# Row halves that wait for TensorE's own semaphore, and the order inside an attention step

## The chip, the cores and the metric

The kernel runs on one core of a Trainium2 chip. TensorE multiplies matrices and writes to PSUM, ScalarE (ACT) and VectorE (DVE) read PSUM, GpSimd (POOL) works on SBUF alone, and SyncE (SP) issues most of the DMAs. Each engine works off its own queue in order and meets the others at semaphores. In the profile PE stands for matmuls and PEld for the weight loads in front of them. The metric is the device time of one execution in microseconds. Before the change it is 1590.65 us, the median of three runs (1590.64 to 1590.91).

## The reference, cut to what matters

```python
xn = layernorm(x)                                  # x: (1, 2048, 512)
qkv = xn @ A_wqkv                                  # 32 heads of 16
scores = einsum("bhqd,bhkd->bhqk", q, k) * 16 ** -0.5
p = softmax(scores)
s = (einsum("bhqk,bhkd->bhqd", p, v) -> (1, 2048, 512)) @ A_wo
g = silu(gelu(xn @ B_w1 + B_b1) @ B_w2 + B_b2)     # hidden width 1376
out = x + s * g
```

## The kernel before, in words

Operands of the dense products are split into a high and a low part, and each product is the sum of three (high by high, high by low, low by high), so that a contraction over 128 rows is many matmuls into one PSUM bank.

The work has two large parts. In the **dense part** (51 to 476 us) the products for q, k, v, the hidden layer and the gate are computed. Each contraction over 128 rows is cut into two of 64 rows. Row half 0 of TensorE's array takes the upper 64, row half 1 the lower 64, and matmuls of the two halves run side by side. A list named `plan` fixes the order: `quad` computes values, `half(j, 0)` and `half(j, 1)` compute a pair of hidden or query and key tiles (L590, weights w1), and `down` multiplies the hidden tiles by w2 (L590, weights w2). `run` takes one matmul for each half in turn. `fill` slips score matmuls (S, L183) among them, and VectorE takes the maxima of their rows (L189).

A bank is written by one half first and by the other afterwards, for instance `half(j, 0)` gives tile x to half 0 and `half(j, 1)` gives it to half 1. The second writer must wait until the first is done. `mm` keeps the last writer of each bank and a number `seen` up to which all matmuls are known to be done (a score matmul that waits for a free bank raises it too). Where that isn't enough, a **token** serves: `mark` puts a tiny ScalarE instruction on the queue (L604, tile junk, two of them on VectorE, L602) that waits for the latest matmul, and the matmul of the other half waits for the token. Tokens are put down ahead of need, in each `down` after its fourth pair of matmuls (`mark_early`) and at hooks in `quad`.

The **attention part** (476 to about 1550 us) has 512 steps, one for each 128 keys of a unit of four heads by 512 queries. A step has four T, one for each head: the scores, transposed (keys on partitions), by `t_one` at L739, each followed by an exp on ScalarE (L741). T take four banks in turn, three named pst and one named ps; the fourth T of a step takes ps. V at L804 multiplies the exps of the step before by the values, eight matmuls by column quarters. The row maxima for later units are computed beside this by S: one `S` writes a whole bank, `X` writes the left half of one and `Y` the right half; three banks are used in turn, and VectorE reduces each (L189). So a step in this mode has two `S`, one `X` and one `Y`. The string for it is `ORDER[3]`, used in all steps from the third to about the 490th:

```python
ORDER = {0: "TTTTV", 3: "STXTTSTYV"}
```

The first and second T of a step lie on row half 1, the third and fourth on row half 0 (L981); the first S and the X lie on half 0, the second S and the Y on half 1. So the first S and the first T share the array, and so do X and the second T, the third T and the second S, the fourth T and Y. Before Y stands a `nop` on TensorE that waits for X on TensorE's own semaphore, since both write the same bank from different halves.

Small jobs hang on the T of a step (`todo`, by step and position): what is put at position 0, after the first T, are `o_move` (five DMAs), `o_den` (a VectorE reciprocal L832 and two DMAs) and `o_div`; loads and the rest stand at position 3. When the maxima of a unit are complete, `s_end0` runs behind an S: a VectorE reduction (L247), two GpSimd instructions and the loads of a later unit's queries.

Of the kernel before, what the change touches and what calls it, by code (L numbers as in the profile page):

```python
# [8 lines left out]
F32 = mybir.dt.float32  # L9
F32R = mybir.dt.float32r  # L10
AF = mybir.ActivationFunctionType
# [25 lines left out]
FILL0 = 30  # L37
HB = 4
W2B = 2
ORDER = {0: "TTTTV", 3: "STXTTSTYV"}  # L40
HC = CH // 2
PAIRED = 28
KB = 3
# [5 lines left out]
def fused(ctx: ExitStack, tc: tile.TileContext, x, wqk, wv, wo, w1, b1, w2, b2, out):  # L49
    nc = tc.nc  # L50
# [17 lines left out]
    ident_r = keep.tile([P, P], F32R, name="ident_r")  # L68
# [17 lines left out]
    SYNC = mybir.DependencyInfo(mybir.DependencyClass.Sync, mybir.DependencyReason.DATA)  # L86
# [68 lines left out]
    done = {u: 0 for u in range(NU)}  # L155
# [106 lines left out]
    prog = {}  # L262
# [42 lines left out]
    for i in range(nu):  # L305
        pairs.append(ms[2 * i:2 * i + 2])
        if (i + 1) * len(qs) // nu > i * len(qs) // nu:
            g, c = qs[i * len(qs) // nu]
            pairs.append([("q", g, c), ("q", g, c + 1)])
    parts = [(c, f, h) for c in range(NCH) for f in range(FT) for h in range(2)]  # L310
    is_m = [pair[0][0] == "m" for pair in pairs]
    plan, nd = [("first", g, i) for g in range(VQ - 1) for i in (0, 2)], 0
    for j in range(len(pairs)):
        for h in range(2):
# [9 lines left out]
            n = 2 if nd < len(parts) and parts[nd][2] and ready - nd > room else 1  # L324
            n = max(n, need - 2 * (left - 1))
            while nd < ready and n > 0:
                c, f, k = parts[nd]
# [9 lines left out]
    def w1_load(j):  # L337
        if j < len(pairs):
            for u in pairs[j]:
                kind, n, f = u  # L340
                if kind == "m":
                    W1[u] = w_new(w1[f], 2, "raw1")
                elif f % 2 == 0:
                    W1[n] = w_new(wqk[:, n], 2, "raw1")

    def w1_split(j):
        if j < len(pairs):
            for u in pairs[j]:
                u = u if u[0] == "m" else u[1]
                if not isinstance(W1[u], tuple):  # L350
                    W1[u] = w_split(W1[u], "w1", 4)

    def w2_load(i):
        if i < len(ms):
            W2[ms[i][1:]] = w_new(w2[ms[i][2]], 2, "raw2")

    def w2_split(i):
        if i < len(ms):
            W2[ms[i][1:]] = w_split(W2[ms[i][1:]], "w2", W2B)
# [27 lines left out]
    def v_out(t, pv):  # L387
        dst = vsb[:, t, :H * VW].rearrange("p (h w) -> p h w", w=VW)[:, :, :DH]
        nc.scalar.activation(dst, pv.rearrange("p (h w) -> p h w", w=DH), AF.Copy)
# [148 lines left out]
    keep_r = ctx.enter_context(tc.tile_pool(name="keep_r", bufs=1, side="right"))  # L538
# [19 lines left out]
    writer = {}  # L558
    s_when, put, row = [], [0], [0, 0]
# [3 lines left out]
    def fill(a):  # L563
        due = FILL0 + put[0] + sum(made) * ROWS // (4 * LEAD)
        if sum(made) < 4 * LEAD and row[a] >= due and (made[0] <= made[1]) == (a == 0):
            taken()
            if later and later[0][0] <= 0:
                put[0] += 2
                u = later.pop(0)[1]
                s_end1(u)  # L570
                s_end2(u)
                return
            s_one(a)
            row[a] += 1
            tick()
# [6 lines left out]

    def mm(a, key, ps, lhs, rhs, first, last):
        r = slice(64 * a, 64 * a + 64)
        token = None
        if not first and writer[key][0] != a and writer[key][1] > prog["seen"]:
            if not tokens or tokens[-1][0] < writer[key][1]:
                mark()
            prog["seen"], token = next(x for x in tokens if x[0] >= writer[key][1])
        i = nc.tensor.matmul(ps, lhs[r], rhs[r], start=first, stop=last).ins  # L590
        if token is not None:
            tc.add_manual_dep(i, token, SYNC, reason="other row tile")
        prog["pe"] += 1
        row[a] += 1
        latest[0] = (prog["pe"], i.name)
        writer[key] = (a, prog["pe"])

    tokens, latest = [], [None]

    def mark(dve=False):  # L600
        if dve:
            i = nc.vector.tensor_copy(junk[:, 1:], ident_r[:1, :1].bitcast(F32)).ins  # L602
        else:
            i = nc.scalar.activation(junk[:, :1], ident_r[:1, :1].bitcast(F32), AF.Copy).ins  # L604
        tc.add_manual_dep(i, latest[0][1], SYNC, reason="row tile done")
        tokens.append((latest[0][0], i.name))

    def mark_early(n):
        if prog["seen"] < n:
            mark()  # L610

    junk = keep_r.tile([1, 2], F32, name="junk")

    def run(ops, hooks={}):
        for n, two in enumerate(zip(*ops)):
            prog["n"] += 1
            for a in range(2):
                fill(a)
                mm(a, *two[a])
            for h in hooks.get(n, []):  # L620
                h()
# [3 lines left out]
    def terms(u, a, begin):  # L625
        kind, n, f = u
        c = f if kind == "q" else n
        out = []
        for k in range(KT):
            for i, j in ((0, 0), (0, 1), (1, 0)):  # L630
                if kind == "v":
                    lhs, rhs = (xh, xl)[i][c][:, k, f * P:(f + 1) * P], (wv_h, wv_l)[j][:, k]
                else:
                    w = W1[u if kind == "m" else n]
                    lhs, rhs = w[i][:, k * P:(k + 1) * P], (xh, xl)[j][c][:, k]
                out.append([u, PH[u], lhs, rhs, False, False])
        if begin:
            out[0][4] = True
        else:
            out[-1][5] = True  # L640
        return out
# [3 lines left out]
    def down(c, f, part):  # L645
        i = c * FT + f
        if f == 0 and part == 0:
            PA[c] = [ps_v.tile([P, D], F32, name="pv")] + [ps_t.tile([P, D], F32, name="pst") for t in range(3)]
        h, w = HS[c, f], W2[c, f]
        side = (part + i) % 2  # L650
        ops = [[], []]
        for a in range(2):
            for t in ((0, 1), (2, 3))[(a + side) % 2]:
                ts = slice(t * P, (t + 1) * P)
                for n, (x, y) in enumerate(((0, 0), (0, 1), (1, 0))):
                    ops[a].append(((c, t), PA[c][t], h[x][:, ts], w[y],
                                   f == 0 and part == 0 and n == 0, f == FT - 1 and part == 1 and n == 2))
        n = prog["pe"]
        if (c, f, part) == parts[-2]:
            run(ops, {2: [lambda: mark(True)], 5: [lambda: mark(True)]})  # L660
        else:
            run(ops, {3: [lambda: mark_early(n)]})
        if part == 0:
            w2_split(i + 1)
            w2_load(i + 3)
            return
        del HS[c, f], W2[c, f]
        if f == FT - 1:
            for t in (0, 2, 1, 3):
                gt = wk.tile([P, D], F32, name="gt", bufs=4)  # L670
                if c == NCH - 1:
                    nc.vector.tensor_add(gt, PA[c][t], b2_sb)  # L672
                else:
                    nc.scalar.activation(gt, PA[c][t], AF.Copy)
                rs = slice(c * CH + t * P, c * CH + (t + 1) * P)
                if c < NCH - 1:
                    chores.append((gt, rs))
                else:
                    nc.gpsimd.dma_start(g_d[rs, :], gt)
# [22 lines left out]
    def quad(n, at):  # L702
        us = first[n]
        for u, b in zip(us, BANKS[n]) if at == 0 else ():
            pool, name = {"x": (ps_x, "ps"), "m": (ps_m, "ps"), "v": (ps_v, "pv"), "t": (ps_t, "pst")}[b]
            PH[u] = pool.tile([P, CH], F32, name=name)
        for i in range(at, at + 2):
            hooks = {6: [mark]} if i in (1, 2) else {}
            if n == VQ - 2 and i in (0, 2):
                hooks[3] = [lambda: w1_split(0) if i == 0 else w1_load(1)]  # L710
            run((terms(us[i], 0, i < 2), terms(us[(i + 2) % 4], 1, i < 2)), hooks)
            if i >= 2:
                for u in (us[i - 2], us[i]):
                    v_out(u[1] * NCH + u[2], PH.pop(u))
# [213 lines left out]
    for u in range(NU):  # L928
        g, c = divmod(u, NCH)
# [17 lines left out]
    for t in range(NW):  # L947
        n = DONE + 2 * t
# [6 lines left out]
    for i, t in enumerate(late):  # L955
        n = L - 2 * len(late) - 1 + 2 * i
# [9 lines left out]
    for n in range(L + 1):  # L966
        ua, ka = divmod(n, 16)
        want = due(n) - due(n - 1)
        i = 0
        for op in ORDER[want] if n > 1 else ("TTTTV", "TTSTSVT")[n]:  # L970
            if op in "SXY":
# [67 lines left out]
```

## Time and profile before

| | |
|---|---|
| median of the runs | 1590.65 us |
| the profiled execution | 1590.04 us |
| its span, first to last instruction | 1588.3 us |
| granted TensorE clock | 1.00 throughout |
| dense part | about 51 to 476 us |
| attention steps with S | about 478 to 1500 us |
| ScalarE busy in 900 to 1100 us | 198.17 us of 200 |
| VectorE busy in 900 to 1100 us | 183.02 us of 200 |

A row of the timeline gives start, length, engine, line, operation, output<-inputs, and, in brackets, how long the engine was idle ahead of it and what ended that. Neighbouring rows of one kind are merged (x2, x3). A wait row gives the total, the number and the longest. PE's busy time counts a matmul from its start to a modelled end, with the filling and emptying of the array, and these overlap from one matmul to the next.

### The profile page before, as it was taken

How to read it: one execution, taken by the hardware profiler on the slowest of the kernel's cores; microseconds unless marked ns; L12 is line 12 of the kernel's file. 1: busy time of each engine (PE TensorE's matmuls, PEld its weight loads, DVE VectorE, ACT ScalarE, POOL GpSimd, SP SyncE). 2: the span in 40 equal slices, each digit the busy share in tenths (PEclk: the TensorE clock that was granted, in tenths of full speed). 3: DMA queues.
4: the chain of work that ended last, by engine and by line, in shares of the span. 5: the costliest groups of instructions: out<-in, count | busy, mean ns of one | idle time of the engine just before them, and what ended most of it. 6: DMA issues, size and time to landing. Idle time of an engine off the chain costs nothing.

```text
span 1588.3 us, 31761 instructions
## 1 busy us (share of the span) xinstructions
PE 1581.8 (100%) x12144; PEld 934.7 (59%) x12144; DVE 1379.1 (87%) x2261; ACT 1259.1 (79%) x2520; POOL 373.7 (24%) x394
## 2 busy tenths in 40 slices
PE   9999999999999999999999999999999999999998
PEld 8899999999894444444444444444444444444445
DVE  7599898989889999999999999999999999999734
ACT  4334343434349999999999999999999999999984
POOL 4145575756640011001000100100100000000143
PEclk9999999999999999999999999999999999999999
DMA  6626343454332123112410511411150111110252
GB/s 206 150 59 161 109 137 99 157 139 134 114 96 59 37 42 59 28 38 47 76 31 25 70 41 30 62 39 29 33 76 21 32 29 36 36 29 22 59 192 101
DMA packets 74648, 116.87 MB, mean 74 GB/s; under 512 B 23012, under 2 KB 24292, under 8 KB 73320
## 3 DMA queue, kind: packets, MB, share of 16 engines
q1 hardware_dynamic: 70748, 101.89, 23.7%
q0 software_dynamic: 3264, 12.35, 4.5%
q8 instruction: 96, 1.57, 0.4%
q10 hardware_dynamic: 484, 0.60, 0.1%
q14 instruction: 56, 0.46, 0.1%
HBM read 84.35 MB, written 25.97 MB: 69 GB/s over the span
## 4 chain that ended last, share of the span: by engine, by line
PE 97%; ACT 1%; DVE 1%; issue 0%; DMA 0%; ACTq 0%; DVEq 0%
PE pv L804 33%; PE ps L183 24%; PE ps L590 12%; PE pst L739 10%; PE pst L590 7%; PE ps L739 3%; PE ps L80 3%; PE pv L590 2%; PE ps L458 1%; ACT slot L741 1%; PE pst L80 1%; DVE st L417 0%; PE pst L440 0%; DMA xt<-in_x 0%; PE pst L458 0%
## 5 line engine op out<-in xcount | busy, mean ns | idle before, releaser
L189 DVE TENSOR_REDUCE mx<-ps 128x2 f32<-128x512 f32 x2048 | 1299.5, 684 | 144.6 <-PE pst L739 35.2
L741 ACT ACTIVATE slot<-pst 128x512 f32<-128x512 f32 x1533 | 831.7, 614 | 17.8 <-PE pst L739 9.6
L804 PE MATMUL pv<-slot,vsb 128*32 128x512 f32 x4096 | 545.4, 605 | 0.0
L183 PEld LDWEIGHTS ps<-kt,slot 48*128 48x128 f32 x1364 | 223.8, 184 | 280.2 <-DVE mx L189 278.3
L183 PE MATMUL ps<-kt,slot 48*128 48x512 f32 x1364 | 379.4, 365 | 0.0
L739 PE MATMUL pst<-qt,kt 50*128 50x512 f32 x1149 | 376.0, 436 | 0.5 <-DVE gt L672 0.3
L741 ACT ACTIVATE slot<-ps 128x512 f32<-128x512 f32 x515 | 316.5, 615 | 2.5 <-PE ps L183 0.2
L590 PE MATMUL ps<-slot,w1h 64*128 64x512 f32 x1088 | 218.1, 393 | 0.0
L739 PEld LDWEIGHTS pst<-qt,kt 50*128 50x128 f32 x1149 | 188.6, 184 | 41.8 <-ACT slot L865 12.6
L183 PE MATMUL ps<-kt,qz 48*128 48x512 f32 x512 | 212.7, 415 | 0.0
L183 PEld LDWEIGHTS ps<-slot,slot 48*128 48x128 f32 x598 | 98.3, 184 | 121.5 <-DVE mx L189 120.7
L183 PE MATMUL ps<-slot,slot 48*128 48x512 f32 x598 | 166.0, 364 | 0.0
L739 PE MATMUL ps<-qt,kt 50*128 50x512 f32 x387 | 162.7, 422 | 0.0
L590 PEld LDWEIGHTS ps<-slot,w1h 64*128 64x128 f32 x1088 | 151.5, 185 | 8.4 <-ACT junk L604 2.6
L804 PEld LDWEIGHTS pv<-slot,vsb 128*32 128x32 f32 x4096 | 80.8, 108 | 109.2 <-issue 100.2
L590 PE MATMUL ps<-slot,w1l 64*128 64x512 f32 x544 | 141.9, 393 | 0.0
L377 POOL TENSOR_TENSOR hl<-hg,hh 128x512 fp32r<-128x512 f32 x76 | 96.8, 1295 | 129.7 <-ACT hh L376 85.9
L250 POOL CAST nmh<-nm 128x16 fp32r<-128x16 f32 x32 | 6.3, 196 | 477.4 <-DVE nm L247 409.3
L739 PE MATMUL pst<-qt,slot 50*128 50x512 f32 x384 | 113.4, 421 | 0.0
L604 ACT ACTIVATE junk<-ident_r 1x1 f32<-1x1 f32 x92 | 18.0, 196 | 116.5 <-PE pst L590 113.3
L183 PEld LDWEIGHTS ps<-kt,qz 48*128 48x128 f32 x512 | 93.8, 183 | 16.3
L842 POOL TENSOR_TENSOR ot<-ot,dn 64x512 f32<-64x512 f32 x15 | 19.6, 1304 | 299.7 <-DMA dn<-den_d 256.9
(159 smaller groups left out, 1757.7 us busy)
## 6 DMA issues: line engine op xcount, KB each, us to landing
raw<-in_w SPq DMA_DIRECT2D x88, 256.0 KB
qk_h<-hh SPq DMA_DIRECT2D x32, 256.0 KB
qk_l<-hl SPq DMA_DIRECT2D x32, 256.0 KB
qt<-qk_h SPq DMA_DIRECT2D x128, 64.0 KB
slot<-qk_h SPq DMA_DIRECT2D x92, 64.0 KB
g_d<-gt POOLq DMA_DIRECT2D x16, 256.0 KB, 3.5
qt<-qk_l SPq DMA_DIRECT2D x64, 64.0 KB
dn<-den_d SPq DMA_DIRECT2D x32, 128.0 KB
```

What stands on the lines that cost most here:

```text
L80: nc.tensor.matmul(ps, lhs[a], rhs[b], start=first and n == 0, stop=last and n == 2)
L183: return nc.tensor.matmul(ps[:, c0:c0 + w], QS[u][r, p, qi * P:(qi + 1) * P], kts[u // NCH % KB][p][r, k0:k0 + w], start=True, stop=True).ins
L189: nc.vector.tensor_reduce(MX[u][:, 2 * p:2 * p + 2, qi, ki][:, heads, parts], ps.rearrange("p (n c) -> p n c", c=HC), axis=AX.X, op=OP.max)
L250: nc.gpsimd.tensor_copy(hl[:, 0], nm)
L377: nc.gpsimd.tensor_sub(hl, raw, hh.bitcast(F32))
L458: nc.tensor.matmul(pq["q", g, c], W1[g][i][:, k * P:(k + 1) * P], (xh, xl)[j][c][:, k], start=n == 0 and k == 0, stop=n == 2 and k == KT - 1)
L590: i = nc.tensor.matmul(ps, lhs[r], rhs[r], start=first, stop=last).ins
L604: i = nc.scalar.activation(junk[:, :1], ident_r[:1, :1].bitcast(F32), AF.Copy).ins
L739: nc.tensor.matmul(ps, kts[g % KB][p][r, k * P:(k + 1) * P], QT[u][r, p, :], start=True, stop=True)
L741: nc.scalar.activation(PT[u, k][:, 2 * p + a, :], ps, AF.Exp, scale=SCALE)
L804: nc.tensor.matmul(PV[u][32 * j:32 * j + 32, :], vsb[:, k, h:h + 32], PT[u, k][:, j, :], start=(k == 0), stop=(k == NT - 1))
L842: eng.tensor_mul(ot[c][rs, g // 2], ot[c][rs, g // 2], DN.pop(u)[rs])
```

## The change

Tokens disappear. Where a matmul must wait for the other half, a `nop` on TensorE waits for the bank's last writer on TensorE's own semaphore; `seen` then rises to that writer and not to a later matmul. `mark`, `mark_early`, the tile junk and all hooks that put tokens down go. Apart from that, the first T and the first S of a step change places in `ORDER[3]`.

```diff
-ORDER = {0: "TTTTV", 3: "STXTTSTYV"}
+ORDER = {0: "TTTTV", 3: "TSXTTSTYV"}
...
-        token = None
         if not first and writer[key][0] != a and writer[key][1] > prog["seen"]:
-            if not tokens or tokens[-1][0] < writer[key][1]:
-                mark()
-            prog["seen"], token = next(x for x in tokens if x[0] >= writer[key][1])
+            hold = nc.tensor.nop().ins
+            tc.add_manual_dep(hold, writer[key][2], SYNC, reason="other row tile")
+            prog["seen"] = writer[key][1]
         i = nc.tensor.matmul(ps, lhs[r], rhs[r], start=first, stop=last).ins
-        if token is not None:
-            tc.add_manual_dep(i, token, SYNC, reason="other row tile")
         prog["pe"] += 1
         row[a] += 1
-        latest[0] = (prog["pe"], i.name)
-        writer[key] = (a, prog["pe"])
+        writer[key] = (a, prog["pe"], i.name)
...
-        n = prog["pe"]
-        if (c, f, part) == parts[-2]:
-            run(ops, {2: [lambda: mark(True)], 5: [lambda: mark(True)]})
-        else:
-            run(ops, {3: [lambda: mark_early(n)]})
+        run(ops)
...
-            hooks = {6: [mark]} if i in (1, 2) else {}
+            hooks = {}
```

More of the change, by code (lines that the diff above doesn't have):

```diff
@@ L584, in mm @@
         r = slice(64 * a, 64 * a + 64)
-        token = None
         if not first and writer[key][0] != a and writer[key][1] > prog["seen"]:
-            if not tokens or tokens[-1][0] < writer[key][1]:
-                mark()
-            prog["seen"], token = next(x for x in tokens if x[0] >= writer[key][1])
+            hold = nc.tensor.nop().ins
+            tc.add_manual_dep(hold, writer[key][2], SYNC, reason="other row tile")
+            prog["seen"] = writer[key][1]
         i = nc.tensor.matmul(ps, lhs[r], rhs[r], start=first, stop=last).ins
-        if token is not None:
-            tc.add_manual_dep(i, token, SYNC, reason="other row tile")
         prog["pe"] += 1
         row[a] += 1
-        latest[0] = (prog["pe"], i.name)
-        writer[key] = (a, prog["pe"])
[L598 to L602, printed above, removed]
-        else:
[L604 to L612, printed above, removed]
+        writer[key] = (a, prog["pe"], i.name)
     def run(ops, hooks={}):
@@ L657, in down @@
                                    f == 0 and part == 0 and n == 0, f == FT - 1 and part == 1 and n == 2))
-        n = prog["pe"]
-        if (c, f, part) == parts[-2]:
-            run(ops, {2: [lambda: mark(True)], 5: [lambda: mark(True)]})
-        else:
-            run(ops, {3: [lambda: mark_early(n)]})
+        run(ops)
         if part == 0:
```

## The prediction

> **What bounds the kernel now.** I read the page first, then the waits, then one stretch of the timeline in each of the two parts that the change touches.
>
> ```profile
> PE 1581.8 (100%) x12144; PEld 934.7 (59%) x12144; DVE 1379.1 (87%) x2261; ACT 1259.1 (79%) x2520; POOL 373.7 (24%) x394
> ...
> PE pv L804 33%; PE ps L183 24%; PE ps L590 12%; PE pst L739 10%; PE pst L590 7%; PE ps L739 3%; PE ps L80 3%; PE pv L590 2%; PE ps L458 1%; ACT slot L741 1%; PE pst L80 1%; DVE st L417 0%; PE pst L440 0%; DMA xt<-in_x 0%; PE pst L458 0%
> ...
> L604 ACT ACTIVATE junk<-ident_r 1x1 f32<-1x1 f32 x92 | 18.0, 196 | 116.5 <-PE pst L590 113.3
> ```
>
> The page says that TensorE is the bound everywhere, but a matmul's end in it is modelled, so it cannot tell a packed step from one that is held up. The last row is the token: 92 tiny ScalarE instructions, 18.0 us busy, with ScalarE idle 116.5 us ahead of them. ScalarE is not on the chain in that part, so neither figure is a saving. What the tokens cost TensorE stands in the waits (total us, times, longest):
>
> ```profile
> PEld ps L183 <- DVE mx L189: 399.0, 476, 0.8
> ...
> PEld ps L590 <- ACT junk L604: 2.6, 9, 0.4
> ```
>
> Nine waits, 2.6 us. The 399 us above them look like the thing to attack, and are not: 476 times 0.84 us, in which the weight-load path has nothing to load while the eight value matmuls (L804) run. The attention steps show it. Here are two and a half of them, by timeline (start, length, engine); the windows row ahead counts 490 such steps in 1021.92 us, 2.086 us each.
>
> ```profile
> 478.50:1500.42 1021.92, 1021.81 (x7858) 460.96 (x7854) 934.84 (x1536) 1011.37 (x1991) 75.87 (x126) 1.00 0.20 41
> ```
>
> ```profile
> 899.90 0.50 PE L183 MATMUL ps<-kt,slot 48*128 48x512 f32 x1
> ...
> 899.91 0.62 ACT L741 ACTIVATE slot<-ps 128x512 f32<-128x512 f32 x1
> ...
> 900.58 0.18 PEld L739 LDWEIGHTS ps<-qt,kt 50*128 50x128 f32 x1
> ...
> 900.71 0.28 PE L183 MATMUL ps<-kt,slot 48*128 48x256 f32 x1
> ...
> 901.01 1.06 PE L804 MATMUL pv<-slot,vsb 128*32 128x512 f32 x8
> 901.92 0.62 ACT L741 ACTIVATE slot<-ps 128x512 f32<-128x512 f32 x1
> ...
> 902.01 0.50 PE L183 MATMUL ps<-kt,slot 48*128 48x512 f32 x1
> ...
> 902.01 0.73 PE L739 MATMUL pst<-qt,kt 50*128 50x512 f32 x2
> ...
> 902.35 0.27 PE L183 MATMUL ps<-kt,slot 48*128 48x256 f32 x1
> ...
> 902.55 1.89 DVE L189 TENSOR_REDUCE mx<-ps 128x2 f32<-128x512 f32 x3 [0.22 <-PE ps L183]
> 902.58 0.40 PE L183 MATMUL ps<-kt,slot 48*128 48x512 f32 x1
> 902.58 1.57 ACT L741 ACTIVATE slot<-pst 128x512 f32<-128x512 f32 x3
> 902.59 0.18 PEld L739 LDWEIGHTS ps<-qt,kt 50*128 50x128 f32 x1
> 902.68 0.18 PEld L183 LDWEIGHTS ps<-kt,slot 48*128 48x128 f32 x1
> 902.71 0.38 PE L739 MATMUL ps<-qt,kt 50*128 50x512 f32 x1
> 902.82 0.28 PE L183 MATMUL ps<-kt,slot 48*128 48x256 f32 x1
> ...
> 903.03 1.06 PE L804 MATMUL pv<-slot,vsb 128*32 128x512 f32 x8
> ...
> 904.02 0.50 PE L183 MATMUL ps<-kt,slot 48*128 48x512 f32 x1
> ...
> 904.49 0.18 PEld L183 LDWEIGHTS ps<-kt,slot 48*128 48x128 f32 x1
> ...
> 904.60 0.41 PE L183 MATMUL ps<-kt,slot 48*128 48x512 f32 x1
> ```
>
> Steps begin at 899.90, 902.01 and 904.02: 2.11 us, then 2.01 us. From the value matmuls to the next step it is 1.00 us (901.01 to 902.01) and 0.99 us (903.03 to 904.02), so the start of a step waits for nobody. The difference sits in front of the value matmuls: 1.11 us in the long step, 1.02 us in the short one. What is late there is the fourth T, which writes the bank ps. In the long step its weights load at 900.58. The exp that empties this bank ran from 899.91 for 0.62 us, to 900.53, and 0.05 us later the load starts. In the short step the exp ended at 902.54 and the load came at 902.59, which is 0.58 us into the step and just in time. So every second step is held by a loop through ScalarE: first T, its exp, three more exps behind it, then the fourth T of the next step. VectorE is close behind, but has 0.22 us of idle time per step at 902.55.
>
> **The change, part by part: the order in a step.** S and T of a step's first pair lie on different row halves and start together at 902.01, S first in the queue. They don't hand over together. VectorE, idle before, takes S at 902.55, 0.54 us after the start; ScalarE takes T at 902.58, after 0.57 us. This is not a property of ScalarE, as a step without S shows, where a T comes first and ScalarE was idle:
>
> ```profile
> 1530.65 0.73 PE L739 MATMUL pst<-qt,kt 50*128 50x512 f32 x3
> ...
> 1531.19 1.58 ACT L741 ACTIVATE slot<-pst 128x512 f32<-128x512 f32 x3 [0.16 <-PE pst L739]
> ```
>
> 0.54 us again. So the second of two that end together reports 0.03 us later, and the swap turns this round: T's exp comes 0.03 us earlier, S's reduction 0.03 us later. The Trainium skill, page "TensorE: Matmul & The Clock Gate", section "The cost: per-tile semaphore tail", says that completions which each raise a semaphore are written one after another, 26.3 ns each beside 4.7 ns for a further tile; by it the second would be 31 ns late, an estimate from the page, and 245 such gains would make 7.6 us. The trace agrees, at 0.03 us.
>
> What 0.03 us is worth follows from the loop. It closes once in two steps, from a first T to the fourth T of the step after, so a pair of steps (4.12 us now, against 2 x 2.01 = 4.02 us if nothing held it) gets shorter by 0.03 us, as 0.10 us is more than 0.03. 490 steps are 245 pairs: 245 x 0.03 = 7.4 us.
>
> Against it stands VectorE. Its three reductions run from 902.55 for 1.89 us, to 904.44; the second S of the next step, whose bank they free, loads weights at 904.49 and starts at 904.60, 0.58 us into the step, the same place as 902.58 in the short step. It comes just in time, and with reductions 0.03 us later it starts at 0.61. The half-width S behind it stands at 0.81 us (900.71; 902.82) and would stand at 0.84. In the short step 0.21 us lie between it and the value matmuls (902.82, 903.03), so these could start at 0.84 + 0.21 = 1.05 us. The fourth T lets them start at 1.11 - 0.03 = 1.08 us. So the ScalarE loop still ends last, by 0.03 us. That fails where VectorE has one more thing to do:
>
> ```profile
> L247 DVE TENSOR_REDUCE nm<-mx 128x16 f32<-128x128 f32 x32 | 8.8, 276 | 0.1
> ```
>
> Some 30 pairs hold such a reduction of 0.276 us, and there I count no gain: 30 x 0.03 = 0.9 us given back. Bounds for the order: VectorE takes all of it (0) to all 245 pairs gaining (7.4). I take 7.4 - 0.9 = 6.5 us.
>
> The moved T brings its queue work with it: the exp, and in some steps what hangs on the first T, which are o_move's five DMAs and o_den's reciprocal and two DMAs. On SP they now stand ahead of the query loads that a first S may ask for; on VectorE the reciprocal stands ahead of the first reduction, in the 0.22 us of idle time. Nothing on PE waits for these within the step, so I cost them at nothing; without that cover each would delay one reduction by its own length. The half-width X now stands right behind the S of its own half; it starts 0.34 us after it in any case (902.01, 902.35), a few ns either way.
>
> **The dense part.** The trace has nine token waits. The order of the changed program has twelve holds (a TensorE no-op that waits for TensorE's own semaphore) in place of twelve tokens that a matmul waited for; the other 80 tokens were never waited for. One wait, and beside it an undisturbed stretch:
>
> ```profile
> 160.85 0.39 PE L590 MATMUL pst<-w2h,hl 64*128 64x512 f32 x1
> ...
> 161.09 0.39 PE L590 MATMUL pst<-w2h,hl 64*128 64x512 f32 x1
> 161.12 0.20 ACT L604 ACTIVATE junk<-ident_r 1x1 f32<-1x1 f32 x1 [2.12 <-PE pst L590]
> ...
> 161.38 0.18 PEld L590 LDWEIGHTS ps<-slot,w1h 64*128 64x128 f32 x1 [0.33 <-ACT junk L604]
> ...
> 161.72 0.39 PE L590 MATMUL ps<-slot,w1h 64*128 64x512 f32 x2
> ...
> 185.03 0.53 PE L590 MATMUL pst<-w2h,hl 64*128 64x512 f32 x2
> 185.26 0.53 PE L590 MATMUL ps<-slot,w1h 64*128 64x512 f32 x2
> ```
>
> Undisturbed, a half starts a matmul every 0.23 us (185.03, 185.26). Here the half that was behind goes from 161.09 over 161.38 to 161.72, 0.63 us for two such slots of 0.46: 0.17 us lost. The half that was ahead, from 160.85, loses 0.41 us. Nine waits cost 1.5 to 3.7 us; I take 1.5, since the half that is behind ends last.
>
> A hold waits for the last matmul of the other half on that bank itself, not for a token put behind later work: seven pairs back in nine of the twelve, 7 x 0.23 = 1.6 us, against a matmul of 0.39 us. So it finds its semaphore raised. The same construct stands before the second half-width S already: the first starts at 902.35, ends after 0.27 us, and the weights behind the no-op load at 902.68, 0.06 us later, while the matmul begun at 902.58 is still going on. It doesn't empty the array. If a hold cost what a token did, this gain would be 0. Behind a hold stands all of TensorE's queue, but it has the other fourteen matmuls still to issue from. ScalarE's 18.0 us and the two VectorE tokens are off the chain: nothing.
>
> Sum, against this execution's 1590.04 us (span 1588.3): -6.5 - 1.5 = -8.0, so 1582.0. The median of the runs is 0.6 higher, 1590.65: 1582.6 us.
>
> **The rivals.** (1) The 0.03 us belongs to the row half, not to the place. S is always on the first half there, and 1530.65 has no S beside it, so no row excludes it. Then T gains nothing: -1.5, 1589.2 us. The same page of the Trainium skill, section "What overlaps and what doesn't", has matmuls start and end strictly in program order, which speaks for the place; no run here shows a pair the other way round. (2) VectorE takes half of the gain: its slack of 0.03 us is no more than the step, so where steps scatter, it ends last. -3.3 - 1.5: 1585.9 us. (3) The slower one: the later reductions push the second S in each long step, and the value matmuls follow the half-width S there and not the fourth T. It decides once the half-width S stands within 0.21 us of the value matmuls; then each pair loses 0.03 us, +7.4 - 1.5 = +5.9: 1596.5 us. Against it: in the long step they are 0.30 us apart (900.71, 901.01), 0.09 us of room for 0.03. (4) The holds do not do what they say and stall as the tokens did: -6.5, 1584.1 us, inside the range.
>
> **How the numbers follow.** Forecast, with (4): 0.60. (2): 0.18. (1): 0.14. (3): 0.08. The likeliest is 1582.6 us, by itself 1579.5 (all pairs, and 3.7 in the dense part, are -11.1) to 1584.5. For 8 in 10 I go to 1588.0, past (2) and short of (1). A change under 0.2%, 3.2 us, cannot be told from none: faster 0.78, same 0.14, slower 0.08.
>
> **What would show it.** First exp of a step 0.54 us after its T where ScalarE was idle, first reduction 0.57 us after its S; long steps of 2.08 us and short ones still 2.01; the stretch of 490 steps near 1015.4 us; no wait of weight loads on ScalarE in the dense part. Wrong, if long steps stay at 2.11 (1), or if the second S starts 0.61 us or later into most steps and the value matmuls move with it (2, 3).

## The result, and the profile after

The changed kernel takes 1582.61 us, median of six runs (1582.34 to 1583.08), against 1590.64 us (1590.40 to 1590.91) for the kernel before on the same chip: a ratio of 0.9950, 95% interval 0.9937 to 0.9963, or 8.0 us less. The profiled execution took 1582.56 us, its span is 1580.8 us (1588.3 before).

The waits of the whole execution (total us, times, longest), as far as weight loads wait for ScalarE's exps:

```profile
PEld pst L715 <- ACT slot L717: 310.0, 404, 0.8
...
PEld ps L715 <- ACT slot L717: 107.2, 139, 0.8
```

The wait for a ScalarE token is gone from the list, and so is the 399 us wait of S for VectorE. The latter has for the most part only changed its name: the weight loads ahead of the first matmul of a step have nothing to do while the value matmuls run, 0.84 us in most steps (479 of the 543 waits in the two rows are 0.8 us or longer), and the first matmul is a T now. Since it moved to another name with the order of two instructions, this was no wait for the engine named.

The two parts by windows (stretch, its length, then busy us of PE, PEld, DVE, ACT, POOL with their instructions), the 490 attention steps and the dense part from its first to its last row-half matmul; below them the dense part of the kernel before:

```profile
478.00:1492.98 1014.98, 1014.87 (x7858) 472.03 (x7855) 936.98 (x1536) 1009.52 (x1991) 75.85 (x126) 1.00 0.21 41
51.82:474.94 423.12, 423.12 (x3560) 387.36 (x3560) 373.02 (x585) 147.12 (x270) 238.10 (x209) 1.00 0.42 121
```

```profile
51.56:475.53 423.97, 423.97 (x3561) 386.23 (x3560) 373.12 (x587) 160.69 (x361) 239.03 (x209) 1.00 0.42 120
```

The steps lost 1021.92 - 1014.98 = 6.94 us, the dense part 0.85 us. The dense part began 0.26 us later in this execution (51.82 against 51.56), before anything that the change touches, and the three add up to the 7.5 us of the spans within 0.1 us (6.94 + 0.85 - 0.26 = 7.53).

A long and a short step after the change, by timeline:

```profile
884.38 0.62 ACT L717 ACTIVATE slot<-ps 128x512 f32<-128x512 f32 x1
...
884.42 0.49 PE L715 MATMUL pst<-qt,kt 50*128 50x512 f32 x1
...
884.42 0.50 PE L183 MATMUL ps<-kt,slot 48*128 48x512 f32 x1
...
884.91 0.18 PEld L183 LDWEIGHTS ps<-kt,slot 48*128 48x128 f32 x1
884.95 1.57 ACT L717 ACTIVATE slot<-pst 128x512 f32<-128x512 f32 x3
884.99 0.42 PE L183 MATMUL ps<-kt,slot 48*128 48x512 f32 x1
885.05 0.18 PEld L715 LDWEIGHTS ps<-qt,kt 50*128 50x128 f32 x1
...
885.25 0.27 PE L183 MATMUL ps<-kt,slot 48*128 48x256 f32 x1
...
885.48 1.06 PE L780 MATMUL pv<-slot,vsb 128*32 128x512 f32 x8
...
886.47 0.50 PE L715 MATMUL pst<-qt,kt 50*128 50x512 f32 x1
...
886.47 0.50 PE L183 MATMUL ps<-kt,slot 48*128 48x512 f32 x1
...
887.00 1.57 ACT L717 ACTIVATE slot<-pst 128x512 f32<-128x512 f32 x3
887.04 1.89 DVE L189 TENSOR_REDUCE mx<-ps 128x2 f32<-128x512 f32 x3 [0.17 <-PE ps L183]
...
888.49 0.50 PE L715 MATMUL pst<-qt,kt 50*128 50x512 f32 x1
```

T starts at 886.47 and its exp at 887.00, after 0.53 us; S starts at the same time and its reduction follows after 0.57 us (887.04). The two have exchanged their delays. The steps last 2.05 us (884.42 to 886.47) and 2.02 us. In the long one the load of the fourth T still waits for the exp on its bank (884.38 + 0.62 = 885.00, load at 885.05), but 0.63 us into the step, not 0.68. The second S loads at 0.49 us, as soon as VectorE has freed its bank.

The two steps are typical. Each score matmul (T, S, X or Y) adds one to a semaphore of TensorE when it is done, and the trace has the times of these updates: the two of a first pair come 0.034 us apart in the median of 488 steps, before and after the change, and 0.034 to 0.035 us in nine steps of ten. In the median of the steps the first exp started 0.566 us after its T before, and 0.533 us after the change.

### The profile page after: what moved, and what is told of

It is laid out like the page before. It is cut to its first block, busy times and chain, and to the rows that moved or that the text cites. A ratio compares the mean times of both kernels' runs of the same rounds, so it can differ in the third digit from the quotient of the medians.

```text
span 1580.8 us, 31627 instructions
## 1 busy us (share of the span) xinstructions
PE 1573.9 (100%) x12144; PEld 946.8 (60%) x12144; DVE 1381.3 (87%) x2259; ACT 1243.7 (79%) x2428; POOL 372.7 (24%) x394
## 4 chain that ended last, share of the span: by engine, by line
PE 98%; DVE 1%; DMA 0%; issue 0%; ACT 0%; DVEq 0%
PE pv L780 33%; PE pst L715 22%; PE ps L589 12%; PE ps L183 9%; PE pst L589 7%; PE ps L715 7%; PE ps L80 3%; PE pv L589 2%; PE ps L458 1%; PE pst L80 1%; DVE st L417 0%; PE pst L440 0%; DMA xt<-in_x 0%; PE pst L458 0%; DVE slot L75 0%
## 5 line engine op out<-in xcount | busy, mean ns | idle before, releaser
L370 ACT ACTIVATE hg<-ps,b_sb 128x512 f32<-128x512 f32 x44 | 27.8, 684 | 133.6 <-PE ps L589 122.1
L715 PEld LDWEIGHTS ps<-qt,kt 50*128 50x128 f32 x387 | 71.1, 184 | 45.6 <-ACT slot L717 39.9
```

The lines of the kernel that those rows point to most:

```text
L370: nc.scalar.activation(raw, ph.pop(u), AF.Gelu_apprx_tanh, bias=b1_sb[:, u[2]:u[2] + 1])
L715: nc.tensor.matmul(ps, kts[g % KB][p][r, k * P:(k + 1) * P], QT[u][r, p, :], start=True, stop=True)
```

## The experiments

Each was compared with the kernel before on the same chip; the ratio has its 95% interval.

**The order alone.**

```diff
-ORDER = {0: "TTTTV", 3: "STXTTSTYV"}
+ORDER = {0: "TTTTV", 3: "TSXTTSTYV"}
```

> The order of the step alone, tokens as before. If the order carries its share of the forecast, this is 6.5 to 7.5 us under before (490 steps near 1014.4 us instead of 1021.9), and the first exp of a step starts 0.53 to 0.54 us after its T. Rival: the order is worth 0.8 us or less and the two changes only work together; then it is within 1 us of before.

Measured: 1583.02 us, ratio 0.9955 (0.9942 to 0.9967), 7.3 us under before (1590.31). The steps by windows:

```profile
478.46:1493.34 1014.88, 1014.78 (x7859) 472.13 (x7855) 936.92 (x1536) 1009.34 (x1991) 75.90 (x126) 1.00 0.21 41
```

The order alone carries the 7 us, with tokens as before. The rival, that the two changes only work together, falls.

**The holds alone.** The changed kernel with `3: "STXTTSTYV"`.

> The holds alone, order of the step as before. By the forecast 1.5 us under before; by the trace of the changed kernel, in which the dense part from its own start is 0.84 us shorter, 0.8 us. The 490 steps stay at 1021.9 us. Rival: a token wait costs 0.3 to 0.4 us each, and something gives a part back: then 2.6 to 3.7 us, or a stretch of the dense part that is longer than before.

Measured: 1589.55 us, ratio 0.9995 (0.9986 to 1.0004), 0.8 us under before. The interval holds 1, so the time alone shows nothing; the dense part in the trace does, 423.07 us against 423.97:

```profile
51.48:474.55 423.07, 423.07 (x3561) 387.95 (x3561) 373.03 (x585) 147.65 (x270) 238.34 (x209) 1.00 0.42 120
```

In the profiles of the six kernels with holds and full reductions it is 422.69 to 423.12 us, in the four with tokens 423.71 to 423.97. So the gain of 0.9 us is clear, but single profiles of one sort differ by up to 0.4 us. Within that, the two changes add up: 7.3 + 0.8 = 8.1 us, against 8.0 together.

**Place or row half.** The kernel before, S still first, with the halves exchanged in the steps:

```diff
-                    t_one(ua, ka, i % 2, 1 - i // 2)
+                    t_one(ua, ka, i % 2, i // 2)
...
-                s_whole(whole.pop(), 1)
+                s_whole(whole.pop(), 0)
...
-                s_whole(whole[0], 0)
+                s_whole(whole[0], 1)
...
-            x = s_mm(ps, cut[0], 0, 0, cut[1] * HC, HC)
+            x = s_mm(ps, cut[0], 1, HC, cut[1] * HC, HC)
...
-            s_mm(ps, job, 1, HC, n * HC, HC)
+            s_mm(ps, job, 0, 0, n * HC, HC)
```

> The kernel before with the row halves exchanged in every attention step, S still first in the queue: S on half 1, T on half 0. If the place in the queue decides which of two matmuls that end together reports first, nothing changes: T still reports 0.57 us after its start, time within 1 us of before. If the half decides, T now reports after 0.54 us and S after 0.57, and the time is 6 to 8 us under before.

Measured: 1590.16 us, ratio 1.0000 (0.9991 to 1.0008). A step by timeline:

```profile
902.14 0.49 PE L183 MATMUL ps<-kt,slot 48*128 48x512 f32 x1
...
902.14 0.49 PE L739 MATMUL pst<-qt,kt 50*128 50x512 f32 x1
...
902.67 1.89 DVE L189 TENSOR_REDUCE mx<-ps 128x2 f32<-128x512 f32 x3 [0.20 <-PE pst L739]
902.70 1.57 ACT L741 ACTIVATE slot<-pst 128x512 f32<-128x512 f32 x3
```

S is on half 1, T on half 0, and T is late as before: 0.53 us for S, 0.56 for T. The place in the queue decides, not the half: the two updates of the semaphore are 0.034 us apart here as well.

**Second, but not ending together.** The kernel before with `3: "XTSTTSTYV"`.

> The half-width X first, then T, then S: T is second in the queue, but ends alone, since X ends a quarter microsecond earlier. If only two that end together stand in each other's way, T reports after 0.54 us though it is second; if being second costs, 0.57 us. VectorE pays: its first whole reduction starts some 0.11 us later, which is more than the room of 0.03 us that the forecast gave it, so by the forecast's third rival the second S slips to about 0.68 us into the step and the step is bound by VectorE: the time no better than before, or up to 15 us slower. If VectorE has more room than that, 6 us faster.

Measured: 1595.59 us, ratio 1.0034 (1.0021 to 1.0046), 5.3 us slower. A long step:

```profile
902.14 0.62 ACT L741 ACTIVATE slot<-ps 128x512 f32<-128x512 f32 x1
...
902.16 0.39 PE L183 MATMUL ps<-kt,slot 48*128 48x256 f32 x1
...
902.17 0.50 PE L739 MATMUL pst<-qt,kt 50*128 50x512 f32 x1
...
902.70 1.57 ACT L741 ACTIVATE slot<-pst 128x512 f32<-128x512 f32 x3
902.75 0.18 PEld L183 LDWEIGHTS ps<-kt,slot 48*128 48x128 f32 x1 [0.17 <-DVE mx L189]
...
902.80 0.18 PEld L739 LDWEIGHTS ps<-qt,kt 50*128 50x128 f32 x1
...
903.09 0.28 PE L183 MATMUL ps<-kt,slot 48*128 48x256 f32 x1
...
903.30 1.06 PE L804 MATMUL pv<-slot,vsb 128*32 128x512 f32 x8
```

T is second and its exp starts after 0.53 us all the same: it is the neighbour that ends at the same time that costs 0.03 us, not the second place. And VectorE takes over: the load of the second S waits for it until 0.59 us into the step, the half-width Y follows at 903.09, and the value matmuls start 0.21 us after that, at 1.14 us. The fourth T does not hold them: it loads 0.04 us after the exp on its bank (902.14 + 0.62 = 902.76, load at 902.80), and the 0.43 us that lay between its load and the value matmuls in the long steps of the other two kernels (900.58 to 901.01; 885.05 to 885.48) would end at 903.23. This is the third rival of the prediction, brought about by giving VectorE its first whole bank some 0.11 us later (the delay that was expected) in place of 0.03.

**What a hold costs.** The changed kernel with 116 holds more:

```diff
-        if not first and writer[key][0] != a and writer[key][1] > prog["seen"]:
+        if not first and writer[key][0] != a:
```

> The changed kernel with a hold at every hand-over of a bank in the dense part, whether or not the writer is known to be done: 116 holds more. If a hold that finds its semaphore raised costs nothing, the time is within 0.5 us of the changed kernel (near 1582.5). If it costs what lies between neighbouring weight loads around the no-op of the attention steps at most, some 18 ns, it is 2 us slower; if it stops TensorE's queue as a token wait did, 10 us or more.

Measured: 1582.46 us, ratio 0.9949 (0.9937 to 0.9962); the dense part 423.01 us:

```profile
51.74:474.75 423.01, 423.01 (x3560) 386.77 (x3560) 372.96 (x585) 147.49 (x270) 238.20 (x209) 1.00 0.42 120
```

A hold that finds its semaphore raised costs nothing that shows. The trace tells how it was carried out: in most places there is no instruction of its own, and the weight load behind it has the wait in its operands (120 such loads in the dense part, against 8 in the changed kernel; the other 4 are separate waits on TensorE's queue).

**Tokens that nobody waits for.** The order and the holds of the changed kernel, with `mark`, `mark_early` and their hooks kept.

> The changed kernel, but with ScalarE and VectorE still doing the tokens that nobody waits for now. If the tokens cost only through the wait of a matmul, this is within 0.3 us of the changed kernel. If the relief of ScalarE's queue carried a part of the 0.8 us of the dense part, it is up to 0.8 us slower than the changed kernel.

Measured: 1582.54 us, ratio 0.9949 (0.9936 to 0.9963), the time of the changed kernel. ScalarE's relief is worth nothing that shows.

**Where the rest of the token waits went.** The kernel before, and the kernel with holds alone, both with the reductions of the dense part cut to half of the columns (so half of the scores is left out of those maxima) and the exps scaled by an eighth:

```diff
-        nc.vector.tensor_reduce(MX[u][:, 2 * p:2 * p + 2, qi, ki][:, heads, parts], ps.rearrange("p (n c) -> p n c", c=HC), axis=AX.X, op=OP.max)
+        src = ps.rearrange("p (n c) -> p n c", c=HC)
+        if "seen" in prog:
+            src = src[:, :, :HC // 2]
+        nc.vector.tensor_reduce(MX[u][:, 2 * p:2 * p + 2, qi, ki][:, heads, parts], src, axis=AX.X, op=OP.max)
...
-        nc.scalar.activation(PT[u, k][:, 2 * p + a, :], ps, AF.Exp, scale=SCALE)
+        nc.scalar.activation(PT[u, k][:, 2 * p + a, :], ps, AF.Exp, scale=SCALE / 8)
```

> The kernel before with VectorE's reductions in the dense part cut to half of the columns (half of the scores are left out of those maxima; the exps are scaled by an eighth so that they stay finite). The dense part should get shorter by what score matmuls wait for VectorE there, some 1 to 3 us, and the rest stay. Pair of the next kernel.

> The same cut of the reductions, with holds in place of tokens and the order of the step as before. Theory: of what the token waits cost (1.5 us or more), VectorE gives a part back, since score matmuls catch up with it and then wait for its bank; so with a light VectorE the holds are worth 1.5 to 2.6 us against the kernel with light reductions and tokens. Rival: a token wait costs 0.09 us and no more, and the holds are worth 0.8 us here too.

Measured: 1584.32 us with tokens (ratio to before 0.9961, 0.9949 to 0.9973), 1582.03 us with holds (0.9948, 0.9936 to 0.9961). The dense part with tokens, then with holds:

```profile
51.95:469.72 417.77, 417.65 (x3560) 376.07 (x3560) 246.75 (x587) 160.91 (x362) 238.96 (x209) 1.00 0.42 122
```

```profile
51.86:467.27 415.41, 415.41 (x3561) 397.52 (x3560) 246.48 (x585) 147.76 (x270) 238.26 (x209) 1.00 0.43 123
```

With VectorE light the holds are worth 417.77 - 415.41 = 2.36 us, inside the 1.5 to 2.6 us expected; with VectorE as it is they are worth 0.9. So with VectorE light the token waits (nine in its list too, 2.8 us) cost 2.4 us, 0.26 each. If they cost the same with VectorE as it is, 1.5 us of it is given back there; this step is argued, not shown. The groups of weight loads fit it; the last column is idle time ahead of the loads of score matmuls in the dense part, before and with holds alone:

```profile
L183 PEld LDWEIGHTS ps<-kt,qz 48*128 48x128 f32 x512 | 93.8, 183 | 16.3
```

```profile
L183 PEld LDWEIGHTS ps<-kt,qz 48*128 48x128 f32 x512 | 93.7, 183 | 19.1
```

It rises by 2.8 us when the tokens go. With light reductions it is 4.7 us with tokens and 1.6 with holds, so most of the 16.3 us, and all of the rise, comes with VectorE's load. The likely reading: a token wait let VectorE catch up, and without it the next score matmuls wait for VectorE's bank. But idle time of the weight loads is not lost time by itself, as the 399 us showed, so the 2.8 us do not measure what is given back. The light reductions also show what VectorE costs this part at all: 423.97 - 417.77 = 6.2 us, where 1 to 3 us had been expected.

**The second T ahead of X.** The changed kernel with `3: "TSTXTSTYV"`.

> The changed kernel with the second T ahead of X as well. The second pair does not start or end together (X has half the columns), and ScalarE takes the second T 0.48 us after the first whatever its own end. So the place should be worth nothing here: within 0.5 us of the changed kernel (1582.5). If each place ahead is worth 0.03 us to a T, 3 us or more faster.

Measured: 1617.34 us, ratio 1.0171 (1.0156 to 1.0186), 27 us slower than before, which no branch foresaw. A step:

```profile
902.67 0.39 PE L715 MATMUL pst<-qt,kt 50*128 50x512 f32 x1
902.68 0.28 PE L183 MATMUL ps<-kt,slot 48*128 48x256 f32 x1
...
903.16 0.18 PEld L183 LDWEIGHTS ps<-kt,slot 48*128 48x128 f32 x1
903.16 0.38 PE L183 MATMUL ps<-kt,slot 48*128 48x256 f32 x1
...
903.47 1.06 PE L780 MATMUL pv<-slot,vsb 128*32 128x512 f32 x8
```

X runs from 902.68 to 902.96. Y, behind its no-op, would have followed 0.06 us after that in the kernel before; here it loads at 903.16, 0.20 us after X, and 0.10 us after the end of the second T (902.67 + 0.39 = 903.06), which has nothing to do with Y's bank. The updates of TensorE's semaphore explain it. In the kernel before, an update comes within 0.04 us of X's end in each of 488 steps. Here it does in none of them: the next two come at 903.08 and 903.11, after the end of the second T, and Y loads 0.04 us after the second of them, as it does after X's update in the kernel before (902.64, load at 902.68). So X is reported done only after the T that stands ahead of it in the queue, although by its record it ended 0.10 us earlier.

**Y ahead of the fourth T.** The changed kernel with `3: "TSXTTSYTV"`.

> The changed kernel with Y ahead of the fourth T. In long steps the fourth T waits for its bank until 0.63 us into the step and Y stands behind it in the queue; ahead of it Y starts when its half is free. If the value matmuls follow the fourth T alone, nothing changes: within 0.5 us of the changed kernel. If Y behind the waiting T was a second thing that ended last, up to 5 us faster; and if the hold in front of Y (it waits for X, to 0.68 us) now holds the fourth T up, up to 10 us slower.

Measured: 1607.06 us, ratio 1.0106 (1.0089 to 1.0123). The last of the three branches, and more than it gave:

```profile
904.14 0.62 ACT L717 ACTIVATE slot<-ps 128x512 f32<-128x512 f32 x1
...
904.26 0.50 PE L715 MATMUL pst<-qt,kt 50*128 50x512 f32 x1
...
904.61 0.28 PE L183 MATMUL ps<-kt,slot 48*128 48x256 f32 x1
...
904.95 0.18 PEld L715 LDWEIGHTS ps<-qt,kt 50*128 50x128 f32 x1
...
905.38 1.06 PE L780 MATMUL pv<-slot,vsb 128*32 128x512 f32 x8
```

The fourth T loads at 0.69 us here, behind the hold of Y, and at 0.67 to 0.69 us in nearly all steps; the value matmuls start at 1.12 us, and no step is under 2.09 us any more. The exp on its bank had ended at 904.14 + 0.62 = 904.76, 0.19 us before the load. X ended at 904.61 + 0.28 = 904.89, TensorE's semaphore was updated at 904.90, Y loaded at 904.94 (0.04 us after the update, as in nearly all steps), and the fourth T right behind it. A hold whose semaphore is not yet raised stops the weight loads of the other half behind it too. How early Y would have loaded here without the hold was not tried.

## Why the prediction was right, point by point

- **The start of a step waits for nobody, and every second step is held by ScalarE's loop:** right. The time from the value matmuls to the next step is 0.99 us as before (885.48 to 886.47), and it is the long steps that became shorter. Of the 489 steps that can be measured from start to start, 43 take 2.2 us or more, before and after. Of the other 446, 240 were over 2.045 us before, with a median of 2.09 us; 217 are after the change, with a median of 2.06 us.
- **The second of two that end together reports 0.03 us later:** right, and with the mirrored halves and X first settled as the prediction had it, by place and by the common end. Its first rival, the half, falls. So does the second, VectorE taking half of the gain, by the sum that follows.
- **245 pairs of 0.03 us less 0.9 for VectorE's other work, 6.5 us:** the steps gave 6.94 us in the changed kernel and 7.04 with the order alone, so the 0.9 was taken too large, by about half. It does belong where the prediction put it. Step by step in the two traces, the 30 steps with a reduction at L247 and the steps right behind them, 52 in all, gained 0.24 us together (0.35 with the order alone), where 0.03 us for each pair would have made 0.8. The other 437 steps gained 6.71 us, which is 0.031 us for each pair. The long step was forecast at 2.08 us and is 2.05 here; the long step that the forecast read, 2.11 us, was longer than most (their median was 2.09).
- **VectorE's room:** right, and as narrow as said. The second S was forecast to load 0.50 us into a long step and does at 0.49, the half-width S to stand at 0.84 and stands at 0.83, the value matmuls at 1.08 and they come at 1.06. The slower rival was real and at most 0.08 us away: X first, with 0.11 us in place of 0.03, took that step.
- **The dense part, 1.5 us:** the term that was mis-sized. It gave 0.85 us. The prediction priced a wait at 0.17 us, since "the half that is behind ends last". With VectorE light the runs show 0.26 us for a wait, inside its bounds of 1.5 to 3.7 us for all nine; with VectorE as it is only 0.1 us for each is left. That the rest goes to score matmuls that wait for VectorE is likely from these runs but not shown. The prediction did not look at VectorE in this part.
- **Holds and idle ScalarE cost nothing:** right, by 116 holds more and by tokens that nobody waits for.

The mechanism of the larger term was right. That the sum of 8.0 us was met within 0.1 us is luck: one term was 0.5 us too small and the other 0.7 us too large.

## What to carry to other kernels

Where two matmuls end at the same time, give the first place in the queue to the one whose reader lies on the loop that sets the step; before counting on it, look at how much room the other reader has. A wait of TensorE on its own semaphore was free here where it was satisfied when it was reached (116 more of them cost nothing that shows), and stopped the weight loads of both row halves where it was not (1607.06 us). What stands ahead of the writer in the queue matters too, since the writer was reported done only after it (1617.34 us). And a stall that is taken away may be worth less than it lasts when another engine is nearly full: 2.4 us with VectorE light, 0.9 us with VectorE as it is.

## What the runs showed of the hardware that was not expected

Exchanging X and the second T, two instructions of different halves and banks, cost 35 us (1617.34 against 1582.61), through the hold that stands four places later: the load behind it came 0.20 us after the end of its own writer, where it had been 0.06 us, because X's update of the semaphore waited for that T's. Two matmuls that end together make their updates 0.034 us apart, in the order of the queue.
